# A fused attention and feed-forward kernel: two more products computed densely, and all operations in a new order

## The chip, the cores and the metric

The kernel runs on one core of a Trainium2 chip. The metric is the device time of one execution in microseconds (us), the median of several runs. A core has these engines: TensorE (PE; its weight loads are listed apart as PEld), VectorE (DVE), ScalarE (ACT), GpSimd (POOL) and SyncE (SP), which here issues nearly all DMAs. Each engine works through its own queue in the order in which the program issues instructions to it.

## The reference

```python
# q, k, v: (8, 8, 576, 64) float32; w_in: (512, 2048); w_out: (2048, 512)
theta = pi / 2 * arange(S) / S
phi(x) = concatenate([max(x, 0) * cos(theta), max(x, 0) * sin(theta)], -1)   # 128 features
kv  = einsum('bhsf,bhsd->bhfd', phi(k), v)          # per batch and head
z   = phi(k).sum(over s)
num = einsum('bhsf,bhfd->bhsd', phi(q), kv)
den = einsum('bhsf,bhf->bhs', phi(q), z)[..., None] + 1e-6
x   = (num / den) as (4608 tokens, 512)
h   = x @ w_in
out = max(0.01 * h, h) @ w_out                      # (4608, 512) float32
```

## The kernel before

**Groups.** The 4608 tokens go in nine groups of 512: group 0 to 7 hold the first 512 tokens of each of the eight batches, and group 8 the last 64 of every batch. For each group there is an attention part, a *first product* (512 tokens x 512 by 512 x 2048, with the leaky ReLU behind it) and a *second product* (512 x 2048 by 2048 x 512). All matmuls take float16 and sum in float32 in PSUM, which has eight banks of 128 x 512 values.

**Attention.** `q` and `k` steps (`q2.3.c`: group 2, token column 3, cosine) read a loaded float32 stage and write the features in float16 (L246 on DVE or POOL, L244 on ACT); `v` steps cast v. `K2` sums k times v for batch 2 into PSUM, `kv2` copies it out, `N2.j` multiplies with q, `D2.j` divides, `X2.j` (or a DMA, `Tx`) transposes to `xT`, `xc2.j` copies. `Tq` transposes q by a DMA. For the groups 0 and 1 the steps come in halves a and b, and `T`, `tc` transpose q on PE.

**Products.** A dense product is 64 matmuls of 512 columns. In group 0 the first product is dense: `M` steps (L665) and eight activations `a`. All other first products go by seven products of quarters instead of eight (Strassen's scheme in Winograd's form): `P{g}.{u}.{n}`, four units u of seven products n, each four matmuls of 256 columns (L763), 112 in all. `Xs{g}.n` (DVE) form sums of the quarters of `xT`, `Ws` those of the weights. Between the products of a unit stand the steps `b`, `s`, `u` (copies out of and into PSUM, on ACT or DVE) and `y`, `z` (sums, on DVE), and four activations `a`, `c`, `d`, `e` of half width. The second products are formed likewise: `S{g}.n` sums of the activated values G, `Tw` sums of the weights, `F{g}.{n}.{tt}.{h}` with four matmuls of 256 columns each (L852), then `t1`, `t2`, `t3`, `r` on DVE or ACT, and the stores `st`. Group 0's second product is split over its 2048 rows: the first 1024 go densely (`E{tt}.i`, L688, copied to `osb` by `ec`), the last 1024 by seven products (`F0.n.tt.1`, 56 matmuls), added to `osb` by steps `d0` and `r0`.

**Order.** The string `ORDER` lists some 1450 operations by name, with the engine behind a colon, and the program issues them in this order. `L..` are loads from memory. There are four stage buffers for q, k, v and weights in turn, so a load waits until the buffer's former content has been read. `idle.5.14.0` is 14 matmuls on zeros ahead of the real work. `split.h`, `split.n` and `join.n` change whether two PSUM banks are one tile or two.

Of the kernel before, what the change touches and what calls it, by code (L numbers as in the profile page):

```python
# [21 lines left out]
q0b.3.s:D q0a.1.s:A Lv0b k0b.7.c:D q0b.3.c:A q0a.3.s:D q0a.0.s:A q0b.2.c:P q0b.2.s:D q0a.3.c:A k0b.3.c:A
idle.4.11.1 T0.3 v0.1:A q0b.0.s:A q0a.0.c:D T0.1 k0b.0.c:P k0b.2.c:P T0.0 kp0.0.c:D q0a.2.c:P touch kp0.1.s:D
v0.0:A kp0.0.s:D kp0.1.c:D q0a.2.s:A tc0.1:D k0b.5.c:D k0b.8.c:A k0b.6.c:D tc0.0:D k0b.4.c:A kp0.2.s:D v0.3:P
Lw1.0 idle.5.2.2 K0a cw1.0:P kv0a:A v0.2:P T0.2 N0a.0 tc0.3:A tc0.2:D D0a.0 idle.5.6.3 K0b Lw1.2 Lw1.6 N0a.1
Lw1.1 Lw1.8 Lw1.3 kv0b:A N0b.0 X0a.0 D0a.1 idle.2.2.4 N0b.1 D0b.0 xc0a.0:A X0a.1 idle.2.2.5 X0b.0 M2.0.0
cw1.1:A M0.0.0 M1.0.0 M2.0.1 M0.0.1 xc0a.1:D M3.0.0 M3.0.1 xc0b.0:A D0b.1 cw1.3:D M2.1.0 Lw1.5 M2.1.1 cw1.6:P
Lw1.4 M1.0.1 cw1.2:A M3.1.0 cw1.5:P M0.1.0 M3.1.1 M0.1.1 M1.1.0 M2.0.2 X0b.1 xc0b.1:D M1.1.1 M2.0.3 M0.0.2
M0.0.3 Lq1 M1.0.2 M1.0.3 M0.1.2 cw1.4:D Lw1.7 M3.0.2 M0.1.3 M3.0.3 Ws0.1:D cw1.8:A Ws0.2:D M1.1.2 Ws0.4:D
M1.1.3 a0 M2.1.2 M4.0 Lw2.0 M2.1.3 q1.2.c:D M5.0 Lk1a M3.1.2 M3.1.3 a1 q1.0.s:D M6.0 M7.0 M6.1 M7.1 q1.1.s:D  # L30
M8.0 q1.0.c:D a3 cw1.7:D M8.1 M9.0 Lw2.1 M4.1 Lk1b M9.1 Ws0.3:D q1.3.s:A q1.3.c:A Ws1.1:D M10.0 M5.1 M10.1
M11.0 a4 q1.1.c:D M11.1 Ws1.2:D a2 M12.0 a5 cw2.0.0:D cw2.0.1:A M12.1 q1.2.s:A cw2.1.1:P M13.0 Lv1a M13.1
M14.0 M14.1 a6 M15.0 M15.1 a7 k1b.4.c:P E2.0 E2.1 E3.0 Ws1.4:D kp1.0.c:D cw2.1.0:A T1.0 T1.1 v1.0:P tc1.1:A
kp1.1.s:D E1.0 E0.0 kp1.0.s:D kp1.1.c:D Lk4n tc1.0:D T1.2 Lv1b kp1.2.s:D T1.3 k1b.0.c:A Tw1.0:D E3.1 v1.1:A
tc1.2:D k1b.5.c:P tc1.3:A E0.1 K1a Ws1.3:D k1b.7.c:P E2.2 kv1a:A S0.1h:D N1a.1 k1b.2.c:A k1b.6.c:A E2.3 N1a.0
# [5 lines left out]
P1.1.2 k2.4.c:P P1.2.1 s1.1:A P1.1.6 a1.1 c1.0 u1.1:A Tw3.1:D b1.2:D Xs1.4:D F0.1.0.1 Lq3 S0.3h:D P1.1.3
F0.1.1.1 q2.2.c:A z1.1:D Lv2 q2.0.c:D k2.3.s:A P1.0.4 Tw4.1:D P1.2.6 q2.3.s:P P1.2.2 d1.0 P1.1.7 k2.4.s:A
k2.0.s:D y1.1:D t1.0:A F0.6.0.1 u1.2:A e1.1 F0.6.1.1 t2.0:D F0.2.0.1 a1.2 k2.3.c:P s1.2:A d0.4:D d0.3:D b1.3:A
P1.2.7 P1.1.4 F0.2.1.1 z1.2:D F0.7.0.1 S0.4h:D P1.3.5 F0.7.1.1 P1.3.6 k2.2.c:A c1.1 Tq2.0 k2.1.c:A r0.2:D
P1.2.3 y1.2:D F0.5.0.1 P1.3.2 u1.3:A v2.0:A s1.3:A c1.2 F0.5.1.1 v2.1:P t3.0:D k2.1.s:P d0.5:D k2.2.s:A P1.3.7
Tq2.1 Lk3 F0.4.0.1 S1.1l:D F0.4.1.1 P1.2.4 e1.2 d1.2 r0.5:D k2.0.c:D y1.3:D c1.3 F0.3.0.1 F0.3.1.1 d1.1 P1.3.3
r0.4:D join.n Lv3 r0.3:D P1.3.4 a1.3 z1.3:D S1.2l:D e1.3 S1.1h:D K2 d1.3 F1.1.0.0 kv2:A q3.2.s:A q3.1.s:A
q3.0.s:A F1.6.0.0 F1.1.0.1 S1.3l:D N2.0 F1.1.1.0 S1.2h:D q3.0.c:P F1.1.1.1 Lv3n D2.0 F1.6.0.1 t1.1:A q3.3.s:P
F1.6.1.0 st0.2 N2.1 S1.3h:D q3.3.c:A k3.2.s:P F1.6.1.1 D2.1 F1.2.0.0 t2.1:D F1.2.0.1 st0.3 k3.3.c:A q3.1.c:A
q3.2.c:A Lk3n v3.1:P N2.2 D2.2 Tw4.0:D F1.2.1.0 k3.0.s:A F1.7.0.0 Lq4 F1.2.1.1 F1.7.0.1 N2.3 k3.1.c:A D2.3  # L50
F1.7.1.0 r1.2:A F1.7.1.1 F1.5.0.0 X2.0 k3.2.c:A X2.1 t3.1:D X2.2 X2.3 v3.0:A S1.4l:D F1.5.0.1 xc2.0:D k3.1.s:A
k3.3.s:P F1.4.0.0 xc2.1:A F1.5.1.0 S1.4h:D P2.0.1 F1.4.0.1 Lk4 xc2.2:A k3.0.c:D xc2.3:D F1.5.1.1 b2.0:A
k3.4.c:A P2.0.2 Xs2.1:D Xs2.2:D P2.0.5 P2.0.6 Xs2.3:D k3.4.s:P K3 k4.0.s:P Tq3.0 a2.0 r1.5:D u2.0:A s2.0:D
P2.1.1 kv3:A Xs2.4:D z2.0:D P2.0.7 Tq3.1 k4.0.c:D P2.0.3 k4.1.s:D k4.4.c:A F1.3.0.0 N3.0 Lv4 k4.3.c:P k4.2.s:A
F1.3.0.1 y2.0:D P2.1.5 P2.0.4 e2.0 b2.1:A q4.1.c:A D3.0 P2.1.6 s2.1:A u2.1:A q4.0.s:P N3.1 q4.3.c:D D3.1 Lv4n
P2.1.2 P2.1.3 q4.1.s:P q4.3.s:D P2.1.7 F1.4.1.0 z2.1:D d2.0 F1.3.1.0 a2.1 c2.0 y2.1:D v4.0:P P2.2.5 N3.2
k4.3.s:A e2.1 v4.1:P D3.2 P2.2.1 F1.4.1.1 P2.1.4 b2.2:A P2.2.6 k4.2.c:D s2.2:A u2.2:D N3.3 d2.1 st0.4 P2.2.2
c2.1 a2.2 P2.2.3 F1.3.1.1 P2.2.7 D3.3 st0.5 k4.4.s:A Lq5 q4.0.c:P P2.3.5 k4.1.c:A z2.2:D e2.2 y2.2:D P2.3.1 K4
S2.1l:D b2.3:A c2.2 P2.3.6 P2.3.2 u2.3:A r1.3:D Tx3 q4.2.c:A s2.3:D a2.3 S2.2l:D Tq4.0 P2.2.4 r1.4:D P2.3.7
y2.3:D F2.6.0.0 P2.3.3 F2.1.0.0 d2.2 z2.3:D q4.2.s:A P2.3.4 P3.0.1 d2.3 Xs3.1:D Xs3.2:D e2.3 c2.3 Tq4.1 b3.0:A  # L60
# [916 lines left out]
```

## Time and profile before

| what | value |
|---|---|
| median of 3 runs | 277.11 us (277.1 to 277.85) |
| profiled execution: time | 279.91 us |
| profiled execution: span from first to last instruction | 278.1 us |
| mean granted TensorE clock | 0.992 |
| busy: PE, PEld, DVE, ACT, POOL | 266.3, 232.6, 225.9, 192.9, 99.3 us |
| DMA | 57.08 MB, mean 205 GB/s |

The busy times are those of the profiled execution. Matmuls are pipelined, so a busy PE isn't PE at its peak; the step from one matmul to the next tells the rate. Times in timelines count from the first instruction.

### The profile page before, as it was taken

The numbers are of one execution on the slowest core, as the hardware profiler recorded it, in microseconds if no ns is written. First come the engines' busy times: TensorE is split into PE (matmuls) and PEld (weight loads), VectorE is DVE, ScalarE is ACT, GpSimd is POOL, SyncE is SP. The second block draws the span as 40 slices with busy tenths as digits, with TensorE's granted clock in tenths as the row PEclk, the third lists the DMA queues.
The fourth block names the chain that finished last, engine by engine and source line by source line (L and its number), as shares of the span: only waits on it lengthen the run. The fifth ranks groups of instructions, "written<-read, shape, count | busy, mean of one in ns | idle before, by whom it ended". The sixth has DMA issues, their size and how long they took to land.

```text
span 278.1 us, 7012 instructions
## 1 busy us (share of the span) xinstructions
PE 266.3 (96%) x2813; PEld 232.6 (84%) x2813; DVE 225.9 (81%) x443; ACT 192.9 (69%) x342; POOL 99.3 (36%) x72
## 2 busy tenths in 40 slices
PE   6999999699999999999999999999999999999994
PEld 2566567498889999999999899989999999999983
DVE  1987989789999899989968998879878659866752
ACT  6757998599987887777868788647755555655400
POOL 4631062899375833963544265007100000000000
PEclk9999999799999999999999999999999999999999
DMA  6999999969899999999997996694455206101224
GB/s 231 382 390 383 374 304 347 290 201 247 265 286 170 323 212 230 335 170 261 294 333 127 245 175 217 131 213 116 82 106 154 79 2 151 57 21 40 77 61 131
DMA packets 88145, 57.08 MB, mean 205 GB/s; under 512 B 53808, under 2 KB 83504, under 8 KB 87600
## 3 DMA queue, kind: packets, MB, share of 16 engines
q1 hardware_dynamic: 87504, 56.11, 74.5%
q10 hardware_dynamic: 608, 0.52, 0.7%
q8 instruction: 22, 0.36, 0.5%
q14 instruction: 11, 0.09, 0.1%
HBM read 36.70 MB, written 9.44 MB: 166 GB/s over the span
## 4 chain that ended last, share of the span: by engine, by line
PE 76%; DMA 10%; DVE 7%; ACT 3%; issue 2%; SPq 1%; DVEq 0%; ACTq 0%
PE h L763 29%; PE o L852 29%; PE h L665 4%; DMA stage<-in_q_dram 3%; DMA stage<-in_v_dram 3%; PE n L562 2%; DMA qpT<-qp 2%; DMA xT<-xs 2%; PE n L474 2%; PE n L852 2%; DVE ext L234 1%; PE h L852 1%; ACT g L783 1%; DVE xs L586 1%; DVE h L234 1%
## 5 line engine op out<-in xcount | busy, mean ns | idle before, releaser
L783 ACT ACTIVATE g<-h 128x512 f16<-128x512 f32 x90 | 51.8, 598 | 28.9 <-PE h L763 14.3
L852 PEld LDWEIGHTS <-g 128*128 128x128 f16 x680 | 65.5, 98 | 7.3 <-issue 0.4
L852 PE MATMUL o<-w,g 128*128 128x256 f16 x504 | 68.6, 273 | 0.2 <-DVE osb L234 0.2
L763 PEld LDWEIGHTS <-w 128*128 128x128 f16 x512 | 55.8, 114 | 4.9 <-issue 3.4
L763 PE MATMUL h<-xT,w 128*128 128x256 f16 x356 | 51.0, 274 | 0.0
L763 PEld LDWEIGHTS <-wext 128*128 128x128 f16 x384 | 42.1, 114 | 1.4 <-issue 0.2
L852 PE MATMUL o<-T,ext 128*128 128x256 f16 x232 | 32.9, 273 | 0.4 <-DVE osb L234 0.4
L246 POOL TENSOR_SCALAR qp<-stage,sin_t 128x512 f16<-128x512 f32 x12 | 25.1, 2096 | 15.2 <-DVE xs L586 8.8
L246 POOL TENSOR_SCALAR qp<-stage,cos_t 128x512 f16<-128x512 f32 (+1 forms) x11 | 20.1, 1832 | 28.7 <-DMA stage<-in_q_dram 20.1
L852 PEld LDWEIGHTS <-ext 128*128 128x128 f16 x272 | 26.2, 98 | 3.6 <-issue 0.6
L234 DVE TENSOR_TENSOR h<-h,u 128x512 f32<-128x512 f32 x31 | 21.5, 694 | 9.3 <-PE h L763 5.9
L763 PE MATMUL h<-X,wext 128*128 128x256 f16 x180 | 26.5, 272 | 0.2 <-ACT h L238 0.2
L246 POOL TENSOR_SCALAR kp<-stage,sin_t 128x512 f16<-128x512 f32 (+1 forms) x9 | 18.1, 2018 | 12.0 <-DMA stage<-in_k_dram 6.2
L783 ACT ACTIVATE g<-y 128x512 f16<-128x512 f32 x32 | 20.3, 635 | 2.0 <-DVE y L234 1.8
L238 ACT COPY u<-h 128x512 f32<-128x512 f32 x23 | 13.5, 589 | 11.7 <-PE h L763 11.4
L234 DVE TENSOR_TENSOR y<-h,s 128x512 f32<-128x512 f32 x29 | 19.8, 682 | 2.3 <-PE h L763 1.6
L586 DVE TENSOR_TENSOR xs<-n,rden 128x512 f16<-128x512 f32 x30 | 20.7, 691 | 1.0
L763 PE MATMUL h<-xT,wext 128*128 128x256 f16 x124 | 18.6, 273 | 0.0
L238 ACT COPY h<-h 128x512 f32<-128x512 f32 x25 | 14.5, 580 | 5.0 <-PE h L763 4.6
L852 PE MATMUL o<-ext,g 128*128 128x256 f16 x128 | 17.9, 273 | 0.0
L763 PE MATMUL h<-X,w 128*128 128x256 f16 x116 | 17.4, 272 | 0.1
L246 POOL TENSOR_SCALAR kp<-stage,cos_t 128x128 f16<-128x128 f32 (+2 forms) x12 | 16.9, 1411 | 1.1 <-DMA stage<-in_k_dram 0.8
(144 smaller groups left out, 467.0 us busy)
## 6 DMA issues: line engine op xcount, KB each, us to landing
out_dram<-osb SPq DMA_DIRECT2D x32, 256.0 KB, 3.0
stage<-in_q_dram SPq DMA_DIRECT2D x7, 1024.0 KB, 7.7
stage<-in_k_dram SPq DMA_DIRECT2D x6, 1024.0 KB, 7.1
...
```

The costliest lines, as they stand in the source:

```text
L234: eng.tensor_tensor(out=o, in0=a, in1=b, op=how)
L238: nc.scalar.copy(o, i)
L246: eng.tensor_scalar(out=o, in0=i, scalar1=0.0, scalar2=col, op0=ALU.max, op1=ALU.mult)
L474: nc.tensor.matmul(ps[:, h // NC, (h % NC) * NE : (h % NC + 1) * NE], lhsT=kps[sl, s, :], rhs=vms[sl, s, :], start=start, stop=stop, skip_ ...
L562: nc.tensor.matmul(pairs["n"][lo:hi, h // 4, (h % 4) * NE : (h % 4 + 1) * NE], lhsT=qpT[j // 2][:, j % 2, h, lo:hi], rhs=kv[b][:, h, :],)
L586: nc.vector.tensor_tensor(out=o, in0=ps[:, :, 0 : 4 * NE].rearrange("p a (b e) -> p a b e", e=NE)[:, :, :, 0:D], in1=r.rearrange("p (a b) ...
L665: nc.tensor.matmul(ps[:, m % 2, lo:hi], lhsT=w1[m // 4, c // 2][:, c % 2, m % 4 : 512 : 4], rhs=xT[0][:, lo // P : hi // P, c, :], start=( ...
L763: nc.tensor.matmul(ps[:, mi * HT : (mi + 1) * HT], lhsT=a[:, c, 2 * r0 + mi : 512 : 4], rhs=b[:, c], start=(n in (1, 5) and mi == 0 and c ...
L783: nc.scalar.activation(G[g % 2][:, m : m + 2, r * HT : (r + 1) * HT], {"a": A, "c": y22, "e": E, "d": B_}[e].rearrange("p (m t) -> p m t", ...
L852: nc.tensor.matmul(ps[:, tt], lhsT=a[:, i, tt * P : (tt + 1) * P], rhs=b[:, i], start=(first and i == at and (apart or tt == 0)), stop=(i ...
```

## The change

Group 0's second product is now wholly dense: `E{tt}.0` to `E{tt}.7`, 64 matmuls of 512 columns, copied out by `ec` and stored in four stores `st0.tt` of whole rows. Its sums `S0`, products `F0` and the steps `t`, `d0`, `r0` are gone. Group 1's first product is wholly dense as well: 64 matmuls `H{m}.{c}` and eight activations `ha`, in the two PSUM pairs `h0` and `h1` in turn; `P1`, `Xs1` and its steps in between are gone. The steps `split.n` and `join.n` go, and `split.h` comes later. The order of all operations is another one, from the first load to the last store.

```diff
 ORDER = """
-setup blank:D Lq0b q0b.0.c:P Lk0b q0b.1.s:A Lq0a idle.5.14.0 k0b.1.c:A q0b.1.c:A kp0.3.s:D q0a.1.c:A Lk0a Lv0a
...
-split.n D1b.1 Xs1.1:D cw2.2.0:A Lk2n D1b.0 X1b.1 cw2.3.0:P P1.0.1 ec1:A P1.0.5 xc1b.1:A Xs1.2:D b1.0:A Xs1.3:D
-s1.0:A P1.1.1 X1b.0 P1.0.6 P1.0.3 xc1b.0:D cw2.3.1:P q2.0.s:A P1.0.2 Lk2 u1.0:A P1.0.7 q2.3.c:A Tw1.1:D
...
+Lq0a Lk0a Lq0b setup q0a.0.c:A q0a.2.s:A blank:D q0a.0.s:A kp0.1.s:D q0b.1.c:A kp0.0.c:D kp0.0.s:D Lk0b Lv0a
...
+N0a.0 D0a.0 cw1.0:P N0a.1 K0b Lw1.8 kv0b:A idle.5.1.4 X0a.0 N0b.0 xc0a.0:A D0a.1 Lw1.3 cw1.1:A idle.2.2.5
+N0b.1 D0b.0 X0a.1 idle.4.3.6 M0.0.0 xc0a.1:D M1.0.0 M0.0.1 M2.0.0 D0b.1 X0b.0 M2.0.1 M3.0.0 xc0b.0:D M3.0.1
...
+cw2.2.0:A X1a.1 N1b.0 E1.4 E2.4 E2.5 E1.5 cw2.3.0:P xc1a.0:A D1b.0 xc1a.1:A Lk2 N1b.1 D1b.1 Ws0.2:D q2.2.c:D
+Tw1.0:D q2.0.s:D X1b.0 xc1b.0:A E0.4 E0.5 H0.0 Tw2.0:D Lk2n X1b.1 Lv2n E0.6 xc1b.1:A E2.6 cw2.3.1:A k2.0.s:D
+H0.1 H1.0 q2.3.c:D q2.3.s:D Lv2 H1.1 Lq3 E1.6 H2.0 H2.1 H3.0 ha0 H3.1 H4.0 H4.1 H5.0 ha1 Tw1.1:D Ws0.4:D
+q2.2.s:A Tw2.1:D H5.1 E2.7 k2.2.c:A ha2 H6.0 H6.1 E0.7 q2.1.s:D ec0:A E3.4 E1.7 H8.0 Ws1.2:D E3.5 H8.1 Lk3n
+k2.4.c:A H7.0 H7.1 k2.0.c:A Tw4.1:D E3.6 H9.0 k2.3.s:A q2.0.c:D ha3 H9.1 v2.0:D Ws1.4:D ha4 q2.1.c:D v2.1:D
+Ws0.3:D k2.4.s:A k2.1.c:A E3.7 H10.0 ec1:D k2.1.s:P Tw4.0:D H10.1 H11.0 ec2:A Tw3.1:D k2.3.c:D Tw3.0:D ec3:D
+st0.0 H11.1 H12.0 H12.1 H13.0 ha5 H13.1 H14.0 H14.1 k2.2.s:A H15.0 S1.1l:D Tq2.1 H15.1 ha6 K2 ha7 Tq2.0
+F1.1.0.0 F1.1.0.1 S1.3l:D S1.2l:D Ws1.3:D kv2:A Lk3 q3.1.c:A Lv3n N2.0 q3.2.s:A st0.1 F1.6.0.0 F1.1.1.0
+q3.3.s:P k3.4.s:P F1.1.1.1 S1.1h:D S1.2h:D F1.6.0.1 D2.0 S1.3h:D N2.1 q3.0.c:A F1.6.1.0 q3.0.s:P F1.6.1.1
...
 """
+    def ffn1_second(m, lo, hi, eng):
+        ps = pairs["h0" if m // 2 % 2 else "h1"]
+        for c in range(lo, hi):
+            nc.tensor.matmul(
+                ps[:, m % 2],
+                lhsT=w1[m // 4, c // 2][:, c % 2, m % 4 : 512 : 4],
+                rhs=xT[1][:, :, c, :],
+                start=(c == 0),
+                stop=(c == NKC - 1),
+            )
+
+    def relu1_second(mp, eng):
+        nc.scalar.activation(
+            G[1][:, 2 * mp : 2 * mp + 2, :], pairs["h0" if mp % 2 else "h1"], AF.Lrelu
+        )
...
     def ffn2(tt, lo, hi, eng):
         for m in range(lo, hi):
             nc.tensor.matmul(
                 bank[4 + tt],
                 lhsT=G[0][:, m, tt * P : (tt + 1) * P],
                 rhs=w2[:, m, :],
                 start=(m == 0),
-                stop=(m == NPR - 1),
+                stop=(m == NFT - 1),
             )
+    def store_tile(tt, eng):
+        rows = out[0:MAIN, :].rearrange("(p j) d -> p j d", j=J)
+        nc.sync.dma_start(rows[:, tt], osb[:, tt])
...
-        for i in range(4):
+        for i in range(8):
             op(f"E{tt}.{i}", ffn2, tt, 2 * i, 2 * i + 2)
         op(f"ec{tt}", lambda tt, eng: copy(osb[:, tt], bank[4 + tt], eng), tt)
+        op(f"st0.{tt}", store_tile, tt)
```

The steps `Xs`, `P` and those between the products now begin with group 2, and the steps `S`, `F`, `t`, `r` and the quarter stores with group 1.

More of the change, by code (lines that the diff above doesn't have):

```diff
@@ L20 @@
 ORDER = """
-setup blank:D Lq0b q0b.0.c:P Lk0b q0b.1.s:A Lq0a idle.5.14.0 k0b.1.c:A q0b.1.c:A kp0.3.s:D q0a.1.c:A Lk0a Lv0a
[L22 to L35, printed above, removed]
@@ L41 @@
[L41 to L55, printed above, removed]
@@ L56 @@
[L56 to L60, printed above, removed]
@@ L121 @@
-F8.3.0.1 r8.3.0:D st8.3.0
+Lq0a Lk0a Lq0b setup q0a.0.c:A q0a.2.s:A blank:D q0a.0.s:A kp0.1.s:D q0b.1.c:A kp0.0.c:D kp0.0.s:D Lk0b Lv0a
+idle.5.14.0 q0b.3.c:A q0b.1.s:D q0b.2.c:D q0a.3.c:A q0a.1.s:D kp0.3.s:D q0a.3.s:A k0b.6.c:D k0b.4.c:A
+k0b.3.c:A q0a.1.c:P q0b.0.s:A q0b.0.c:D k0b.2.c:D q0b.2.s:P kp0.1.c:D idle.6.6.1 T0.1 T0.0 k0b.0.c:P touch
+q0a.2.c:A Lv0b q0b.3.s:A T0.2 Lw1.0 k0b.1.c:P k0b.5.c:A v0.0:A tc0.1:A v0.1:P T0.3 tc0.0:D v0.3:P Lw1.2
+tc0.2:A kp0.2.s:D k0b.7.c:A idle.5.5.2 K0a v0.2:A Lw1.6 tc0.3:D Lw1.1 kv0a:D cw1.6:P k0b.8.c:A idle.5.2.3
@@ new lines @@
+N0a.0 D0a.0 cw1.0:P N0a.1 K0b Lw1.8 kv0b:A idle.5.1.4 X0a.0 N0b.0 xc0a.0:A D0a.1 Lw1.3 cw1.1:A idle.2.2.5
+N0b.1 D0b.0 X0a.1 idle.4.3.6 M0.0.0 xc0a.1:D M1.0.0 M0.0.1 M2.0.0 D0b.1 X0b.0 M2.0.1 M3.0.0 xc0b.0:D M3.0.1
+M1.0.1 M2.1.0 cw1.8:P Lw1.5 cw1.2:A M2.1.1 M0.1.0 Lw1.4 M3.1.0 M0.1.1 M1.1.0 cw1.3:A X0b.1 M3.1.1 M2.0.2
+M1.1.1 Lq1 M0.0.2 Lw1.7 M2.0.3 M0.0.3 M3.0.2 xc0b.1:D M1.0.2 cw1.4:D cw1.5:D M1.0.3 M0.1.2 Lw2.0 M0.1.3 M1.1.2
+M3.0.3 M1.1.3 cw1.7:D M2.1.2 M2.1.3 M3.1.2 M4.0 q1.1.s:P q1.1.c:D M5.0 a0 q1.0.s:D M3.1.3 M6.0 q1.3.s:D M7.0
@@ new lines @@
+M4.1 M5.1 Ws1.1:D a1 M6.1 M8.0 M7.1 M8.1 M9.0 M9.1 a3 q1.3.c:A M10.0 a4 M10.1 Lk1a Ws0.1:D M11.0 M11.1 Lw2.1
+M12.0 a5 q1.0.c:D cw2.0.0:D M12.1 M13.0 Lk4n Lk1b M13.1 cw2.0.1:P M14.0 a2 M14.1 M15.0 Lv1a a6 q1.2.s:A M15.1
+a7 T1.0 q1.2.c:A Lv1b v1.0:P kp1.0.s:D kp1.0.c:D E2.0 E0.0 T1.1 E0.1 E1.0 k1b.4.c:P cw2.1.1:D cw2.1.0:A
+kp1.1.c:D E1.1 tc1.1:A E2.1 E2.2 E1.2 tc1.0:D kp1.1.s:D k1b.0.c:D v1.1:A E0.2 T1.2 k1b.7.c:D k1b.3.c:D
+k1b.6.c:A E2.3 Lw2.2 k1b.5.c:P T1.3 k1b.8.c:A E1.3 tc1.2:D kp1.2.s:D K1a E3.0 kv1a:A tc1.3:D v1.2:A N1a.0 E3.1
@@ new lines @@
+t1.1:A F1.2.0.0 k3.0.c:P D2.1 N2.2 Lv3 t2.1:D F1.2.0.1 k3.1.s:P D2.2 F1.7.0.0 Lq4 F1.2.1.0 F1.2.1.1 k3.2.s:A
+k3.2.c:D q3.3.c:A k3.0.s:A q3.1.s:A N2.3 F1.7.0.1 split.h r1.2:A F1.7.1.0 D2.3 F1.7.1.1 Lk5n S1.4l:D k3.3.c:D
+X2.0 X2.1 X2.2 Tq3.0 k3.1.c:A q3.2.c:A X2.3 k3.3.s:A F1.5.0.0 k3.4.c:P F1.5.0.1 t3.1:D xc2.0:A xc2.1:D xc2.2:D
+F1.5.1.0 xc2.3:D P2.0.1 Xs2.1:D v3.0:A b2.0:A F1.5.1.1 P2.1.1 Tq3.1 P2.0.2 P2.0.5 Xs2.2:D Xs2.4:D P2.0.6
+v3.1:A K3 s2.0:A u2.0:A Xs2.3:D a2.0 z2.0:D q4.1.c:D P2.0.7 Lk4 kv3:A P2.0.3 N3.0 P2.1.5 e2.0 Lv4n y2.0:D
@@ new lines @@
+F1.4.0.0 S1.4h:D P2.0.4 b2.1:A Lv4 q4.0.c:D s2.1:A P2.1.6 d2.0 q4.0.s:P u2.1:A P2.1.2 c2.0 st0.3 k4.4.s:P
+F1.4.0.1 D3.0 st0.2 N3.1 P2.1.7 r1.5:D a2.1 F1.3.0.0 P2.2.1 z2.1:D P2.1.3 y2.1:D P2.2.5 q4.1.s:P c2.1 P2.1.4
+e2.1 F1.3.0.1 D3.1 b2.2:A k4.3.s:D N3.2 s2.2:A d2.1 P2.2.6 P2.2.3 F1.3.1.0 k4.0.s:D P2.2.2 u2.2:A F1.3.1.1
+D3.2 k4.4.c:A q4.3.c:A q4.2.s:P F1.4.1.0 a2.2 z2.2:D e2.2 N3.3 P2.3.1 k4.2.s:D P2.2.7 S2.1l:D k4.1.s:P
+k4.3.c:P b2.3:A P2.3.5 k4.1.c:A D3.3 P2.3.6 F1.4.1.1 k4.0.c:A y2.2:D s2.3:D v4.0:P P2.2.4 Lq5 r1.4:D P2.3.2
@@ L122 @@
+F8.5.1.0 S8.4l:D t3.8:D F8.5.1.1 F8.4.0.0 r8.2:A F8.4.0.1 r8.5.0:D F8.4.1.0 st7.4 r8.5.1:D F8.4.1.1 F8.3.1.0
+F8.3.1.1 F8.3.0.0 r8.4:D st7.5 F8.3.0.1 st8.2 st8.5.0 r8.3.1:D st8.5.1 st8.4 r8.3.0:D st8.3.1 st8.3.0
 """
@@ L683 @@
             op(f"a{m // 2}", relu1, m // 2)
+    def ffn1_second(m, lo, hi, eng):
[12 more added lines that the diff above has]
+        )
+    for m in range(NFT):
+        for c in range(2):
+            op(f"H{m}.{c}", ffn1_second, m, 2 * c, 2 * c + 2)
+        if m % 2:
+            op(f"ha{m // 2}", relu1_second, m // 2)
     def ffn2(tt, lo, hi, eng):
@@ L738 @@
             op(f"Ws{bp}.{n}", w1_sum, bp, n)
-        for g in range(1, NG):
+        for g in range(2, NG):
             op(f"Xs{g}.{n}", x_sum, g, n)
     LR = {"a": (0, 0), "c": (1, 1), "e": (0, 1), "d": (1, 0)}
-    FIRST_BANKS = ((4, 5, 7), (6, 3, 4), (0, 1, 6), (2, 3, 0))
     def banks(g, u):
-        if g == 1:
-            return [bank[i] for i in FIRST_BANKS[u]]
         at = 3 * (4 * g + u)
@@ L787, in relu1s @@
         )
-    for g in range(1, NG):
+    for g in range(2, NG):
         for u in range(4):
@@ L814 @@
     G_PARTS = {"l": (0, 4, 1), "h": (4, 8, 1), "e": (4, 8, 2), "o": (5, 8, 2), "x": (0, 8, 1)}
-    for g in range(NG):
+    for g in range(1, NG):
         for n in (1, 2, 3, 4):
@@ L855, in ffn2s @@
                 rhs=b[:, i],
-                start=(first and i == at and (apart or tt == 0)),
+                start=(first and i == 0 and (apart or tt == 0)),
                 stop=(i == NPR - 1 and (apart or tt == 1)),
@@ L864 @@
     QUARTER = {2: (0, 0), 5: (1, 1), 4: (1, 0), 3: (0, 1)}
-    def first_quarter(n):
-        r, c = QUARTER[n]
-        return osb[:, 2 * r : 2 * r + 2, c * HC : (c + 1) * HC]
     def half(t):
@@ L875, in store @@
         cols = slice(c * HC, (c + 1) * HC)
-        if g == 0:
-            o = first_quarter(n)
-        else:
-            o = half(osb[:, (2, 5, 4, 3).index(n)])
+        o = half(osb[:, (2, 5, 4, 3).index(n)])
         if g < B:
@@ L906, in result @@
     def result(g, n, t, eng):
-        o = first_quarter(n) if g == 0 else osb[:, (2, 5, 4, 3).index(n)]
-        if g == 0:
-            tt_op(o, half(flat(g, n)), o, ALU.add, eng)
-        elif t is None:
+        o = osb[:, (2, 5, 4, 3).index(n)]
+        if t is None:
             copy(o, flat(g, n), eng)
@@ L913, in result @@
             tt_op(o, flat(g, n), t, ALU.add, eng)
-    for g in range(NG):
+    for g in range(1, NG):
         for n in range(1, 8):
@@ L930 @@
             op(f"st{g}.{n}", store, g, n)
-            if g == 0 and t is not None:
-                op(f"d{g}.{n}", tt_op, first_quarter(n), first_quarter(n), half(t), ALU.add)
     op("split.h", change, ("h0", "h1"), 2)
-    op("split.n", change, ("n",), 2)
-    op("join.n", change, ("n",), 1)
     engines = {"": None, "D": DVE, "A": ACT, "P": POOL}
```

129 lines of the change are left out of this document (62 added, 67 removed).

## The prediction

> **What bounds the kernel now.** I read the page first, then who waited for whom on TensorE, then the stretch of the longest wait in the timelines, and last the chain through it.
>
> ```profile
> span 278.1 us, 7012 instructions
> PE 266.3 (96%) x2813; PEld 232.6 (84%) x2813; DVE 225.9 (81%) x443; ACT 192.9 (69%) x342; POOL 99.3 (36%) x72
> PEclk9999999799999999999999999999999999999999
> ```
>
> TensorE (PE) is busy for 96% of the span, so a matmul added costs its full time unless it fills a hole. One slice of the clock, the eighth (48.7 to 55.6 us), is not at full speed. The waits of PE, whole run:
>
> ```profile
> PE n L763 <- ACT u L238: 2.3, 1, 2.3
> ...
> PE n L562 <- DMA qpT<-qp: 0.6, 1, 0.6
> PE o L852 <- DVE osb L234: 0.6, 2, 0.4
> ...
> PE n L613 <- DVE xs L586: 0.2, 1, 0.2
> PE h L763 <- ACT h L238: 0.2, 1, 0.2
> ```
>
> The only long one lies in the second group's first product (L763), and it waits for a copy `u` on ScalarE (ACT). What ACT did there, and PE beside it:
>
> ```profile
> 47.61 0.59 ACT L238 COPY s<-o 128x512 f32<-128x512 f32 x1
> 51.00 0.72 ACT L244 ACTIVATE qp<-stage,sin_t 128x512 f16<-128x512 f32 x1 [2.79 <-DMA stage<-in_q_dram]
> 51.62 0.57 ACT L238 COPY u<-n 128x512 f32<-128x512 f32 x1
> ```
>
> ```profile
> 46.18 0.40 PE L598 MATMUL h<-ident,xs 128*128 128x128 f16 x4 [0.24 <-DVE xs L586]
> 46.41 0.60 PE L763 MATMUL o<-xT,w 128*128 128x256 f16 x4
> ...
> 52.24 1.01 PE L763 MATMUL n<-xT,w 128*128 128x256 f16 x4 [2.25 <-ACT u L238]
> ```
>
> `u1.0` stands in ACT's queue behind `q2.0.s`, which needs the third batch's q from memory. ACT waits 2.79 us for it, and PE 2.25 us behind ACT. The clock after the gap:
>
> ```profile
> 50.00:52.20 2.20, 0.00 (x0) 0.00 (x0) 1.11 (x2) 1.20 (x3) 1.10 (x1) 0.96 0.91 246
> 52.20:56.00 3.80, 3.76 (x21) 2.84 (x21) 3.20 (x5) 2.67 (x5) 3.80 (x3) 0.57 1.03 315
> ```
>
> For 3.8 us PE ran at 0.57 of its clock, which loses 0.43 x 3.8 = 1.6 us more than the gap itself. [...]
>
> **The price of a matmul and the size of the stage.** The chain of waits has stretches of back-to-back matmuls, and the two ends of the stage:
>
> ```profile
> 29.18 4.75 PE h L665 x22
> ...
> 41.36 9.55 DMA stage<-in_q_dram
> ...
> 70.30 1.25 PE n L474 x40
> ...
> 243.39 1.75 PE h L763 x16
> ```
>
> A 512-column matmul costs 4.75 / 22 = 0.216 us, a 256-column one 1.75 / 16 = 0.109 us. I take as the stage what lies between 46.18 us (the second group's first transposes; the products follow) and 70.30 us (L474, the sums `K2` of the third batch): 24.1 us. The old order puts all of P1 (4 x 7 x 4 = 112 matmuls of 256 columns) and F0 (7 x 2 x 4 = 56) there, and two `X1b` steps of four transposes, 0.23 us each by the step from 46.18 to 46.41. That is 168 x 0.109 + 0.46 = 18.8 us of work in 24.1 us: 5.3 us are lost, 2.3 in the gap, 1.6 to the clock, 1.4 in small waits.
>
> **The change, part by part.**
>
> Dense products: the first group's second product gets its other half dense, 32 x 0.216 = 6.9 us for F0's 6.1; the second group's first product becomes 64 x 0.216 = 13.8 us for P1's 12.2. PE's own work grows by 2.4 us. The stage then holds 6.9 + 13.8 + 0.46 = 21.2 us, after which PE turns to `K2` as before. With no wait `K2` begins at 46.18 + 21.2 = 67.4 in place of 70.30: **-2.9 us**. This is the main term, and it stands only if the 21.2 us really run dense.
>
> Why they can: P1 needed copies `b`, `s`, `u` and sums `y`, `z` between its products (20 operations on ACT and VectorE, DVE), two or three of them in a chain per unit. The dense H steps need xT, w1 and a free PSUM pair; ACT empties a pair with one `ha`. No instruction that H needs stands behind the q load of 41.36 + 9.55 = 50.9 us: ACT's queue ahead of `ha0` holds only weight casts and `xT` copies. `ha2` alone stands behind `k2.2.c`, whose load lands so:
>
> ```profile
> 44.60 1.04 SPq L289 DMA_DIRECT2D stage<-in_k_dram  x1
> ...
> DMA to landing us min/median/max: 10.1/10.1/10.1
> ```
>
> 44.6 + 10.1 = 54.7 us. H8 needs `ha2`, and 54 dense matmuls (11.7 us) with the transposes stand ahead of H8 in the stage, so PE asks for it at about 58. The cover is some 2 us. A second small wait: E0.6 needs the cast `cw2.3.0` on POOL, which in the old run starts at 47.68:
>
> ```profile
> 47.68 2.22 POOL L240 CAST w<-stage 128x1024 f16<-128x1024 f32 x2 [3.14 <-DMA stage<-in_moe_w_out_dram]
> ```
>
> It is done at 48.8, and PE arrives a little earlier. For it and for PSUM pairs returned late I take **+0.6 us** (0 to 1.5; the upper end is five waits like the small ones of 0.2 to 0.4).
>
> DVE's queue is the new cover to watch. `K2` sums into the pair `n`, which is banks 6 and 7, now held by the dense second product until `ec2` (ACT) and `ec3` (DVE). `ec3` is the 25th operation on DVE from `q2.2.c` on, which waits for 50.9; the fifth, `k2.0.s`, waits for 54.7. From there to the end of `ec3` stand 21: seven of q and k, twelve sums or copies, two casts of v. Steps of DVE with POOL quiet, then beside it:
>
> ```profile
> 26.58 0.87 DVE L246 TENSOR_SCALAR qp<-stage,sin_t 128x512 f16<-128x512 f32 x2
> 27.38 0.48 DVE L246 TENSOR_SCALAR qp<-stage,cos_t 128x512 f16<-128x512 f32 x1
> ...
> 28.37 0.68 DVE L234 TENSOR_TENSOR w<-w,w 128x1024 f16<-128x1024 f16 x1
> 28.98 0.68 DVE L234 TENSOR_TENSOR wext<-w,w 128x1024 f16<-128x1024 f16 x1
> ...
> 30.57 0.69 DVE L240 CAST w<-stage 128x1024 f16<-128x1024 f32 x1
> ```
>
> ```profile
> 58.95 0.77 DVE L246 TENSOR_SCALAR qp<-stage,cos_t 128x512 f16<-128x512 f32 x1
> 59.64 0.68 DVE L234 TENSOR_TENSOR ext<-w,T 128x1024 f16<-128x1024 f16 x1
> ```
>
> Step to step a q operation takes 0.40 alone and 0.69 beside POOL, a sum 0.61. A v cast of 1152 columns I estimate at 0.69 x 1152 / 1024 = 0.78. So `ec3` ends at 54.7 + 7 x 0.40 + 12 x 0.61 + 1.6 = 66.4, or at 68.5 with 0.69. Nearest is a mix, as the new POOL queue has but two operations there (`k2.1.s`, `q3.3.s`): about 67.4, level with PE. It hides, without reserve; no further charge, and the late end goes to the rivals.
>
> Removed with F0: four sums `S0`, three `t`, three `d`, four `r`; with P1: four `Xs1`, the 20 `between` steps. Sixteen half-width `relu1s` become eight full ones. None of it lay on PE's path except through waits already counted. Four stores by quarter become four by rows; the page's stores are 32 of 256 KB before and stay so. They pass SP's queue ahead of `Tq2`, `Lv3` and after `Lv4`; each waits for an `ec` done by 67, so nothing behind them is held: 0.
>
> Start: PE before the first matmul of the first product:
>
> ```profile
> 19.25 0.40 PE L598 MATMUL o<-ident,xs 128*128 128x128 f16 x4
> 19.48 2.09 PE L665 MATMUL h<-xT,w 128*128 128x256 f16 x16
> ...
> 21.41 0.39 PE L598 MATMUL o<-ident,xs 128*128 128x128 f16 x4
> ```
>
> Now `X0b.0` (19.25) has to come first; in the new order four matmuls stand ahead of it, and q and k halves load in another sequence with the same bytes, 33 idle matmuls for 37. Gain between 0 (the same landings decide) and 1.1, or a loss of 0.6 if a preparation falls late on its engine; nearest is the row of the transposes, so **-0.4 us**.
>
> Behind `K2`: all S1 sums now follow `ec3` on DVE. F1.6.0.0 needs the third of them, F1.6.0.1 the sixth, N2.1 the division after it. `ec3` at 67.4 + 6 x 0.61 = 71.1, the division takes a step of 1.03:
>
> ```profile
> 73.95 0.15 DVE L582 TENSOR_SCALAR den<-n 128x8 f32<-128x8 f32 x1
> ...
> 74.98 0.68 DVE L234 TENSOR_TENSOR g<-g 128x1024 f16<-128x1024 f16 x1
> ```
>
> PE with `K2` from 68.0 comes to F1.6.0.1 after 1.25, five pieces of 0.44 and a short one, near 71.7. So a wait of up to 1.5, down to none: **+0.5 us**. From there on the groups have the same matmuls and operations in another order. PE's visible waits after 56 us add up to 1.6 us (the rows above), so a better order can gain at most that; a worse one I bound by the same amount: 0, +-1.6.
>
> Sum: -2.9 + 0.6 - 0.4 + 0.5 = **-2.2 us**. The profiled run has a span of 278.1 and took 279.91; the median of the runs is 277.11. I subtract from the median: **274.9 us**.
>
> **Rivals.**
>
> *The third batch decides anyway* (no change). If the chain of its k and v is what releases `K2`, the saved stall turns into a wait there. DVE at 0.69 per q and k operation, 0.68 per sum and 1.15 per v cast (the row of ACT for that size) ends `ec3` at 54.7 + 4.8 + 8.2 + 2.3 = 70.0; with the 0.5 behind, and no gain from the start since a landing decides, that is 70.0 - 70.3 + 0.5 = +0.2: 277.3. For it: old DVE ran without a pause from 57 to 70. Against: f32 work of P1 and F0 has left that queue.
>
> ```profile
> L238 ACT CAST vm<-stage 128x1152 f16<-128x1152 f32 x2 | 2.3, 1150 | 0.0
> ```
>
> *DVE stands behind POOL* (slower). If DVE stops for the whole of a POOL operation, the two in this stretch cost 2.97 (the row below) and about 2.0: `ec3` at 66.4 + 5 = 71.4, so 71.4 - 70.3 + 0.5 = +1.6: 278.7. It decides from a mean DVE step of (70.6 - 54.7) / 21 = 0.76 us on.
>
> ```profile
> 47.74 1.26 DVE L234 TENSOR_TENSOR xT<-xT 128x512 f16<-128x512 f16 x1
> 48.92 0.41 DVE L240 COPY xT<-h 128x512 f16<-128x512 f16 x1
> ...
> 62.23 2.97 POOL L246 TENSOR_SCALAR kp<-stage,sin_t 128x512 f16<-128x512 f32 x1
> ```
>
> For it: the 1.26 us of a sum on 512 columns beside the casts of 47.68. Against: 0.77 for a q operation under POOL, and 0.67 to 0.68 for sums. [...]
>
> *Everything dense and earlier* (more gain): no new wait (-0.6), nothing behind `K2` (-0.5), the start at its best (-0.7), some of the later 1.6 regained (-0.8): 272.3.
>
> That the dense products don't remove the stall is covered by the first two.
>
> **How the numbers follow.** Forecast 0.56, more gain 0.12, third batch 0.17, POOL 0.15. A difference under 0.3% (0.8 us) can't be told from none. Faster: the first two, 0.68; same: 0.17; slower: 0.15. The likeliest case alone spans 273.3 to 276.2. The range reaches to the best case and to most of the slow one: 272.2 to 278.3.
>
> **What would show it.** The wait on `u` is gone and the eighth slice of the clock is full; L474's third batch starts near 68; PE's work in the stage is 96 matmuls of 0.216. Wrong if PE waits over 1 us at `K2` for DVE, if H waits for `ha2`, or if waits after 75 us exceed 3 us.

## The result, and the profile after

The changed kernel takes 275.7 us (median of 16 runs, 274.63 to 277.19), the kernel before on the same chip 277.76 us (16 runs, 276.46 to 280.27). The ratio is 0.9928, with a 95% interval of 0.9906 to 0.9951: 2.0 us less. The profiled execution took 274.63 us, which is the fastest of its 16 runs. Beside the experiments below the changed kernel ran eleven times more, and the one of these that was profiled took 392.2 us at a granted clock of 0.658, against 274.79 to 277.18 us for the other ten, so it is left out of their ratio, and every view of the changed kernel here is of the execution of 274.63 us. Its head:

```profile
span 272.8 us, 6773 instructions
...
PE 263.0 (96%) x2737; PEld 224.1 (82%) x2737; DVE 216.2 (79%) x432; ACT 179.4 (66%) x308; POOL 103.5 (38%) x71
...
PEclk9999999999999999999999999999999999999998
```

The eighth slice of the clock is full now. DVE has lost 9.7 us of work and ACT 13.5, the copies and sums of P1 and F0. All that the view of PE's waits lists for the changed kernel (engine, line, releaser: total, times, longest):

```profile
PE h L537 <- DVE qp L242: 2.3, 2, 1.9
PE o L374 <- DVE osb L409: 2.2, 1, 2.2
PE h L783 <- DVE u L236: 0.8, 1, 0.8
```

The first two lie ahead of the first product, so from there to the end one listed wait, of 0.8 us, is left. The wait on `u` is gone. The chain of waits of the changed kernel through the stage (start, us, what):

```profile
51.31 3.45 PE h L685 x16
54.76 0.43 PE n L707 x2
...
61.24 5.18 PE h L685 x24
66.42 1.25 PE n L470 x40
```

It is PE alone: 24 dense matmuls of H (L685) in 5.18 us are 0.216 us each, and behind them `K2` (L470) begins at 66.42, where before had 70.30 in the same view. (The timelines and the rows of stretches below give its first matmul, 66.25 and 70.14.) DVE's timeline of the changed kernel tells why nothing holds `K2` (start, us, instruction, in brackets the idle time before):

```profile
52.40 0.49 DVE L242 TENSOR_SCALAR kp<-stage,sin_t 128x512 f16<-128x512 f32 x1 [1.41 <-DMA stage<-in_v_dram]
52.80 0.92 DVE L242 TENSOR_SCALAR qp<-stage,cos_t 128x512 f16<-128x512 f32 x1
53.64 0.48 DVE L242 TENSOR_SCALAR qp<-stage,sin_t 128x512 f16<-128x512 f32 x1
54.04 0.68 DVE L230 TENSOR_TENSOR T<-w 128x1024 f16<-128x1024 f16 x1
...
63.58 0.68 DVE L236 COPY osb<-n 128x512 f32<-128x512 f32 x1
```

The first row is `k2.0.s`, the last `ec3`, which ends at 64.26, 2 us ahead of PE.

### The profile page after: what moved, and what is told of

It is laid out like the page before. It is cut to its first block, busy times and chain, and to the rows that moved or that the text cites. A ratio compares the mean times of both kernels' runs of the same rounds, so it can differ in the third digit from the quotient of the medians.

```text
span 272.8 us, 6773 instructions
## 1 busy us (share of the span) xinstructions
PE 263.0 (96%) x2737; PEld 224.1 (82%) x2737; DVE 216.2 (79%) x432; ACT 179.4 (66%) x308; POOL 103.5 (38%) x71
## 4 chain that ended last, share of the span: by engine, by line
PE 80%; DMA 14%; ACT 3%; DVE 1%; SPq 0%; issue 0%; ACTq 0%
PE o L869 30%; PE h L783 29%; DMA stage<-in_moe_w_out_dram 5%; PE h L685 5%; DMA qpT<-qp 4%; PE n L558 3%; DMA stage<-in_q_dram 2%; PE n L707 2%; PE n L470 2%; DMA xT<-xs 2%; PE o L707 2%; PE h L869 1%; PE n L869 1%; ACT qp L240 1%; PE h L458 1%; ACT qpT L234 1%
## 5 line engine op out<-in xcount | busy, mean ns | idle before, releaser
L869 PEld LDWEIGHTS <-g 128*128 128x128 f16 x640 | 61.8, 98 | 6.5
L803 ACT ACTIVATE g<-h 128x512 f16<-128x512 f32 x84 | 49.1, 598 | 26.9 <-PE h L783 16.4
L869 PE MATMUL o<-w,g 128*128 128x256 f16 x480 | 64.5, 273 | 0.0
L783 PEld LDWEIGHTS <-w 128*128 128x128 f16 x448 | 48.7, 113 | 1.9 <-issue 0.9
L242 POOL TENSOR_SCALAR qp<-stage,sin_t 128x512 f16<-128x512 f32 (+1 forms) x14 | 30.9, 2210 | 39.2 <-DMA stage<-in_q_dram 19.2
L783 PEld LDWEIGHTS <-wext 128*128 128x128 f16 x336 | 36.3, 114 | 0.5
L242 POOL TENSOR_SCALAR kp<-stage,sin_t 128x512 f16<-128x512 f32 (+1 forms) x11 | 20.8, 1895 | 18.4 <-DMA stage<-in_k_dram 16.1
L242 POOL TENSOR_SCALAR qp<-stage,cos_t 128x512 f16<-128x512 f32 (+1 forms) x11 | 22.8, 2074 | 11.5 <-DMA qpT<-qp 7.3
L230 DVE TENSOR_TENSOR osb<-o,ext 128x512 f32<-128x512 f32 x22 | 15.0, 683 | 3.0 <-PE o L869 3.0
L240 ACT ACTIVATE kp<-stage,cos_t 128x512 f16<-128x512 f32 (+2 forms) x27 | 15.3, 586 | 0.0
```

Of the source, the lines that this page charges most:

```text
L230: eng.tensor_tensor(out=o, in0=a, in1=b, op=how)
L240: nc.scalar.activation(o, i, AF.Relu, scale=col)
L242: eng.tensor_scalar(out=o, in0=i, scalar1=0.0, scalar2=col, op0=ALU.max, op1=ALU.mult)
L783: nc.tensor.matmul(ps[:, mi * HT : (mi + 1) * HT], lhsT=a[:, c, 2 * r0 + mi : 512 : 4], rhs=b[:, c], start=(n in (1, 5) and mi == 0 and c ...
L803: nc.scalar.activation(G[g % 2][:, m : m + 2, r * HT : (r + 1) * HT], {"a": A, "c": y22, "e": E, "d": B_}[e].rearrange("p (m t) -> p m t", ...
L869: nc.tensor.matmul(ps[:, tt], lhsT=a[:, i, tt * P : (tt + 1) * P], rhs=b[:, i], start=(first and i == 0 and (apart or tt == 0)), stop=(i = ...
```

## Experiments

All ratios are to the kernel before, run on the same chip beside the experiment, with a 95% interval. Line numbers shift by a few from kernel to kernel; the tiles tell which operation it is.

**How large is the stall in another execution of the kernel before?** No edit.

> The kernel before once more, for a second profile of it. Stall theory (the gain is the wait of PE for the copy u behind the q load, and the slow clock after it): PE waits for u again, but its length follows the landing of the q load; if q lands 2 us earlier than the 50.9 us of the first profile, the wait is near 0.5 us in place of 2.3, and the sums K2 begin near 68 in place of 70.3. Order theory (the gain lies at the start and behind K2, where the new order is better): K2 near 70.3 again, whatever the wait.

277.35 us, near the median of the 22 runs of that kernel on the same chip (277.59), where the execution profiled first took 279.91. PE's clock on the page of this second profile:

```profile
PEclk9999999999999999999999999999999999999999
```

And two of PE's waits in it:

```profile
PE n L763 <- DVE X L234: 0.7, 1, 0.7
PE n L763 <- ACT u L238: 0.6, 1, 0.6
```

ACT's row for `q2.0.s` in it:

```profile
49.55 0.72 ACT L244 ACTIVATE qp<-stage,sin_t 128x512 f16<-128x512 f32 x1 [1.43 <-DMA stage<-in_q_dram]
```

The same q load lets `q2.0.s` start at 49.55, in the first profile at 51.00. With it the wait on `u` shrinks from 2.25 to 0.6 us, and the slow slice of the clock is gone. `K2` begins at 67.69, 2.45 us earlier than in the first profile, which is all of the difference between the two spans (275.6 and 278.1 us). The stall is real, but its size is that of one landing, and the execution that I read had a late one. The stretch from the first matmul of the first product to `K2` shows it as a whole. One row for each execution (start and end, length, then PE busy, PEld, DVE, ACT, POOL, the clock, DMA share, GB/s); first the two profiles of before, the one shown first on top:

```profile
19.48:70.14 50.66, 47.41 (x439) 35.34 (x437) 43.89 (x82) 42.33 (x69) 27.60 (x18) 0.97 0.96 308
```

```profile
19.40:67.69 48.29, 45.98 (x440) 34.78 (x437) 44.53 (x82) 42.04 (x69) 27.23 (x18) 1.00 1.02 323
```

And the changed kernel:

```profile
18.66:66.25 47.59, 47.47 (x369) 27.59 (x368) 37.04 (x73) 32.42 (x45) 14.01 (x10) 1.00 1.05 325
```

PE stands idle for 3.25 and 2.31 us in the kernel before, for 0.12 us in the changed one. Against the second profile the changed kernel has 1.5 us more of PE's work here, 2.2 us less idle time, and starts 0.74 us earlier: 1.4 us in all.

**The change once more, beside the other kernels of this chip.** No edit.

> The changed kernel once more. Both theories: 0.990 to 0.995 of the kernel before; a second profile with K2 at 66 to 67.5 us and no wait of PE over 1 us between 20 us and the last group.

276.05 us (median of all eleven), ratio 0.9932 (0.9902 to 0.9962). The gain repeats in a second set of runs; the second profile of the stage that was asked for did not come of it.

**The wait alone, without dense products.** In the kernel before, the steps of the third batch's q that need the late load go behind `u1.1`:

```diff
-xc1b.0:D cw2.3.1:P q2.0.s:A P1.0.2 Lk2 u1.0:A P1.0.7 q2.3.c:A
+xc1b.0:D cw2.3.1:P P1.0.2 Lk2 u1.0:A P1.0.7
-a1.0 Lv2n q2.1.c:D q2.1.s:P
+a1.0 Lv2n q2.1.s:P
-u1.1:A Tw3.1:D b1.2:D
+u1.1:A q2.0.s:A q2.3.c:A Tw3.1:D q2.1.c:D b1.2:D
```

> The kernel before, with three steps of the third batch's q moved behind the second unit's copies on ScalarE and behind two weight sums on VectorE; the products stay as they were. Stall theory: the wait for u goes and the clock stays full, K2 at 67 to 69, time 274.5 to 276.5; the dense products then are not needed for this part of the gain. Order theory: no change, 277.0 to 278.5. Third: VectorE's chain of sums through this stage takes over and K2 stays at 69 to 70.5, 277 to 278.

276.64 us, ratio 0.9972 (0.9943 to 1.0002). The same stretch:

```profile
19.36:66.73 47.37, 46.06 (x439) 34.62 (x437) 43.60 (x82) 42.04 (x69) 26.63 (x18) 1.00 1.05 327
```

PE's idle time is 1.31 us instead of 2.31, and the stretch is as long as that of the changed kernel (47.37 and 47.59) with 1.4 us less of PE's work. Both rows are of executions below their kernel's median: this one took 275.57 us, 1.1 less, and the changed kernel's lies as far below. By the ratio the three moved steps bring 0.8 us, with an interval that just reaches no change; the time lies between what the two theories asked for, and `K2` at 66.73 is a little ahead of the stall theory's 67 to 69. So once the wait is gone, dense products as such make the stretch no shorter here: what they take out in idle time they put back as work.

**Where the order behind `K2` stands.** The changed kernel up to `ha7 Tq2.0`, then the order of the kernel before:

```diff
 H15.1 ha6 K2 ha7 Tq2.0
-... (order of the changed kernel)
+... (order of the kernel before)
```

> The changed kernel's order up to K2 with its dense products, then the order of the kernel before. Stall theory: it keeps the gain of the changed kernel but for what lies behind K2, 275.0 to 276.5. Order theory: most of the gain is lost, 276.8 to 278.

275.56 us, ratio 0.9927 (0.9899 to 0.9955), the same as the whole change. The stretch:

```profile
18.66:65.95 47.29, 47.29 (x370) 27.61 (x368) 36.14 (x71) 32.37 (x45) 12.67 (x10) 1.00 1.05 330
```

PE isn't idle at all. This kernel was profiled in an execution of 275.49 us, near its median: its `K2` begins 1.74 us earlier than in the second profile of before, and its span is 1.9 us shorter (273.7 and 275.6). So the whole gain lies ahead of `K2`, within the interval of some 0.8 us to either side; the new order of the remaining 207 us is worth nothing that can be measured. The time of the opposite cut (before up to `K2`, then the new order) says nothing of the new order:

> The kernel before up to K2 (with P1 and F0), then the changed kernel's order. Stall theory: 277 to 278.3, no gain beyond noise. Order theory: most of the gain, 275.5 to 276.5.

285.88 us, ratio 1.0329 (1.029 to 1.0369). Its stores of the first group stand behind steps that write the next results to `osb`, so these rows hold other values, and that is what PE waited for:

```profile
PE o L845 <- DVE osb L227: 7.4, 2, 6.9
```

The loss is one of my graft, not of the new order. Up to `K2`, though, this kernel has the order of before, and so its profile is a third one of that stretch: PE waits 0.58 us for `u`, the first product starts at 19.60 and `K2` at 67.72. The late landing of the first profile is the odd one of the three. Start of the first product and of `K2` in all profiles with one order or the other up to there (the last two differ from the changed kernel by one step before `K2` or by none, see below):

| order up to `K2` | first product, us | `K2`, us |
|---|---|---|
| before, first profile | 19.48 | 70.14 |
| before, second profile | 19.40 | 67.69 |
| before, the cut just shown | 19.60 | 67.72 |
| changed kernel | 18.66 | 66.25 |
| changed up to `K2`, then before | 18.66 | 65.95 |
| changed, `k2.2.c` first | 18.73 | 66.42 |
| changed, `Tq6.1` early | 18.25 | 65.74 |

Beside an execution without the late landing `K2` comes 1.3 to 2.0 us earlier, and 0.7 to 1.4 us of that is the earlier start.

**One dense product at a time.** First only H, with F0 kept: P1 and its steps replaced by `H`, `ha` at their places in the old order.

```diff
-P1.0.1 ec1:A P1.0.5 ... (P1, Xs1, b s u y z a c d e)
+ec1:A X1b.1 H0.0 H1.0 ... ha0 ... (H, ha; F0 in its places between)
```

> The kernel before with the second group's first product dense (H) and F0 kept; the order by hand around it, q steps behind the first two activations. Stall theory: PE's work grows by 1.6 us, the wait for u is gone, K2 near 68 to 69: 275.5 to 277.3. Order theory: 277.5 to 279, the added work and no gain.

279.02 us, ratio 1.0081 (1.005 to 1.0112): above what the stall theory asked for, and at the upper end of the order theory's range. The wait for `u` is gone. PE's longest waits behind the start:

```profile
PE h L588 <- DVE xs L576: 1.9, 2, 1.3
PE h L776 <- ACT g L796: 1.2, 1, 1.2
```

A dense H needs the whole of `xT`, and while DVE makes the last of it (`xs`) PE has nothing: in this order no other product stands there, and E is half as long. In the changed kernel the matmuls of E (L707) stand in that place. Then only E, with P1 kept: E in the new order, P1 in the sequence of the third group's P2. The hand-made order doesn't keep every shared value, so part of the output's values differ; the number and size of the instructions are those of the text.

```diff
-H0.0 H0.1 ... ha7
+P1.0.1 b1.0:A ... d1.3 c1.3 (and Xs1.1 to Xs1.4)
```

> The changed kernel with the second group's first product by seven products again (P1, its sums and copies back on ScalarE and VectorE) and the first group's second product dense; the order by hand around it. Stall theory: PE's work is 1.6 us less than in the changed kernel, but waits for copies and sums return, K2 at 68 to 71: 276.5 to 279.5. Order theory: the lower work shows, 274 to 275.3.

284.15 us, ratio 1.0256 (1.022 to 1.0291), above both expected ranges. Its waits of PE, with `K2` at 73.79:

```profile
PE h L778 <- DVE y L225: 3.3, 2, 2.6
...
PE h L778 <- ACT h L229: 2.2, 3, 1.5
PE h L778 <- ACT u L229: 1.0, 3, 0.5
```

The wholly dense E holds the banks `o` and `n` until `ec3`, so P1's units (which use `o`, `n` and `h` in the kernel before, as the rows of L763 in the prediction show) have only `h`, and each copy and sum between the products comes out as a wait. Both single-part kernels are slower than either kernel. My orders for them are made by hand, so they bound little; the two waits they show are of the parts, though: H lacks something to fill with, E takes P1's banks.

**The start alone.** The new order up to `M4.0`, then the kernel before; and the same with the q steps moved as above.

```diff
-setup blank:D Lq0b q0b.0.c:P Lk0b ... (order before, up to M4.0)
+Lq0a Lk0a Lq0b setup q0a.0.c:A ... (new order, up to M4.0)
```

> The kernel before with the changed kernel's order up to the first product's fifth block (M4.0), and its own order from there, P1 and F0 kept. In all profiles so far the first product starts at 18.7 us with the new start and 19.4 with the old. If that is worth its full time: 0.9965 to 0.9985 of the kernel before (0.4 to 1.0 us). If the stage behind waits for loads in any case: 0.999 to 1.001.

> The new start and the three q steps moved behind, P1 and F0 kept: the changed kernel's gain without its dense products. If the gain is the start and the wait for u: 0.992 to 0.9955 of the kernel before, as the changed kernel. If the dense products are needed: 0.996 to 1.0.

280.79 us, ratio 1.0119 (1.0078 to 1.0159), and 280.75 us, 1.0113 (1.0067 to 1.0159): both miss. The first product starts at 18.68, but a new wait follows. DVE's rows and PE's row of the first of the two:

```profile
28.51 0.69 DVE L233 CAST w<-ext 128x1024 f16<-128x1024 f32 x1 [4.00 <-DMA ext<-in_moe_w_in_dram]
29.12 0.68 DVE L227 TENSOR_TENSOR wext<-w,w 128x1024 f16<-128x1024 f16 x1
...
35.03 0.68 DVE L233 CAST w<-stage 128x1024 f16<-128x1024 f32 x1
...
35.77 1.82 PE L681 MATMUL n<-w,g 128*128 128x512 f16 x5 [2.63 <-DVE w L233]
```

The cast of the last weight chunk, `cw1.7`, stands early on DVE in the new start and waits 4.00 us for its load; the sums and features behind it are late, and so is a cast of the second weights that E needs (35.03). DVE in the changed kernel waits as long for that load (4.03 us, to 28.51 too), but PE doesn't wait there: the operations behind it stand in another order, with six of them ahead of the cast that E needs where this kernel has eleven, and the cast starts at 32.70. So I left `cw1.7` where before has it:

```diff
-... cw1.7:D ... M4.0 (in the new start)
+... M4.0 ... cw1.7 (at its place in the order before)
```

> The kernel before with three things of the change and none of its dense products: the order of the start (loads, casts and copies up to the first product), the two quarters of the third batch's q load issued behind the copy of u that they held up, and the cast of the last chunk of the first weights left where before has it on VectorE. Theory A (the change gains by its start, about 0.7 us, and by the wait on u that is gone, 0.6 to 2.5 us; the dense products give back what they cost): ratio 0.991 to 0.9955, first product at 18.7, second stage's first sum at 65.8 to 66.8, no wait of TensorE near 33 us. Theory B (the dense products are needed, since only with them VectorE has the time for the earlier start): ratio 0.996 to 1.0, that sum at 67.5 or later, with waits of TensorE for VectorE before it.

277.3 us, ratio 0.9993 (0.9962 to 1.0025): no gain, though M starts at 18.48 and the q steps are moved. Theory A falls; of theory B the time fits, but `K2` comes at 67.08, ahead of what it asked. So beside the new start the three moved steps show no gain, where alone they gave 0.8 us (-0.1 to 1.6). Where the 0.9 us of the start went is seen at the second batch's first sum of k times v. PE's row in this kernel, then in the second profile of before, then in the changed kernel:

```profile
38.55 0.75 PE L455 MATMUL h<-vm,kp 64*128 64x66 f16 x36 [0.64 <-POOL vm L443]
```

```profile
38.71 0.75 PE L462 MATMUL h<-vm,kp 64*128 64x66 f16 x36
```

```profile
39.90 0.74 PE L458 MATMUL h<-vm,kp 64*128 64x66 f16 x36
```

Without dense products PE comes to it 0.8 us earlier than before and waits 0.64 us for v, so 0.16 of the 0.9 us are left. The changed kernel has 22 matmuls of E between M and this sum, the other two have 14: 8 x 0.216 = 1.7 us of work whose operands are there. PE arrives at 39.90, and v, whose cast on POOL starts 1.0 us later than in the second profile of before (39.01 for 37.99), is ready at 39.68. The second half of E isn't cheaper work; here it is work that fills. That is one wait in one order: no kernel here has P1 and F0 in an order made for the new start, so that only dense products could keep the gain of the start is argued, not shown.

**How near is the cover of `ha2`, and what stands behind?** In the changed kernel the feature `k2.2.c`, which needs the third batch's k, goes ahead of `ha0` on ACT.

```diff
-H2.1 H3.0 ha0 H3.1 ... E2.7 k2.2.c:A ha2
+H2.1 H3.0 k2.2.c:A ha0 H3.1 ... E2.7 ha2
```

> The changed kernel with one step moved on ScalarE: k2.2.c, which needs the third batch's k, stands ahead of the first activation ha0, which empties a PSUM pair that H4 needs. Stall theory: H4 is asked for at 52.5 us, k lands at 52 to 55, so PE waits 1 to 3.5 us for ha0 and the clock falls behind the wait: 277 to 280. Order theory: no change against the changed kernel, 275 to 276.3.

277.5 us, ratio 1.0023 (0.9996 to 1.005). The time lies in the range of the stall theory, but by luck: the expected wait came to 0.2 us (the second row), since k landed at 51.3 us here by the transfers' view, and `K2` starts at 66.42, 0.2 us later than in the changed kernel. Most of the time is lost 100 us later (the first row):

```profile
PE n L551 <- DMA qpT<-qp: 1.9, 1, 1.9
...
PE h L678 <- ACT g L687: 0.2, 1, 0.2
```

The queue of SP in this kernel:

```profile
150.31 0.61 SPq L278 DMA_DIRECT2D stage<-in_k_dram  x1
151.03 0.51 SPq L278 DMA_DIRECT2D stage<-in_v_dram  x1
151.64 9.07 SPq L536 DMA_TRANSPOSE qpT<-qp  x1
```

and in the changed one:

```profile
149.44 0.51 SPq L285 DMA_DIRECT2D stage<-in_v_dram  x1
150.05 7.59 SPq L543 DMA_TRANSPOSE qpT<-qp  x1
```

The transpose of the seventh group's q stands behind the loads of the eighth batch; issued 1.6 us later it occupies the queue until 160.7 instead of 157.6, and PE waits. In both kernels the product that reads it starts 3.6 us after that (164.28 and 161.20), and in the changed one PE stands idle for 0.1 us ahead of it. So the changed kernel sits on an edge at that place. The profile is of an execution of 279.23 us, 1.7 above this kernel's median: against the changed kernel's profile PE is 1.25 us late at `K6`, and 4.73 us at `K7`, behind the wait. Taking the edge away didn't help:

```diff
-k6.4.c:D Lk7n ... Tq6.1 (behind Lk7n, Lk7, Lv7)
+k6.4.c:D Tq6.1 Lk7n ... (and u5.3:D ahead of Xs6.1:D, Xs6.3:D)
```

> The changed kernel with Tq6.1 issued ahead of the eighth batch's loads, and with Xs6.1 and Xs6.3 behind the copy u5.3 on VectorE; all else as it is. The changed kernel waits there for 0.3 us and 0.9 us in its profile, and 2.1 us for Tq6.1 in another. If these are on the path: 0.3 to 1.5 us less than the changed kernel, 0.988 to 0.992 of the kernel before, and a narrower spread of its runs. If PE catches up later: 0.9925 to 0.9935.

275.91 us, ratio 0.9947 (0.9917 to 0.9977), no better than the change itself. That transpose now takes 3.54 us of the queue, and the waits for it and for `u` are gone, but in the profiled execution (277.19 us, 1.3 above the median) others came (0.9 us for `xs`, 0.7 for `y`). No version beat the changed kernel by more than can be measured.

## Why the prediction was right

Forecast 274.9 us, measured 275.7; forecast -2.2 us, measured -2.0. Step by step:

- *The main term, -2.9, was over-sized, and the step that failed is that it was read off one execution and taken from the median of others.* The mechanism held: the wait on `u` is gone and the stage runs dense, with 0.1 us lost in it. Against the execution of 279.91 us the size holds too: the stretch from the first product to `K2` is 50.66 - 47.59 = 3.1 us shorter. But the 2.3 us of stall and 1.6 us of slow clock belong to that execution. Against the one of 277.35 us, near the median, the stretch is 0.7 us shorter, or 1.0 in the kernel cut at `K2`.
- *The added work of +2.4 us is there:* 96 x 0.216 for 168 x 0.109. The rows of the stretch show only +1.5 us of PE's busy time. The rest is probably the modelled end of the last matmul ahead of a gap, which counts as busy: four matmuls are given 0.60 us where their steps take 4 x 0.109 = 0.44, and the second profile of before has six gaps in the stretch (6 x 0.16 = 1.0), the changed kernel one.
- *The +0.6 for E0.6 and the pairs of H was not incurred:* no wait of PE between 18.66 and 66.25.
- *The start, -0.4, was -0.8* (18.66 for 19.48): the row of the transposes was too small a bound for the likeliest value. In the one order tried without the longer E it did not pay (the last start experiment).
- *`ec3` at 67.4 was too late by 3.1 us.* The step of 0.40 for features and 0.60 for sums held, beside POOL too but for the feature at 52.80; the mistake was the release, 54.7 by before's load, 52.40 in the changed kernel, whose k load is issued earlier (42.83 for 44.60). From `k2.0.s` to the end of `ec3` it is 11.9 us, by the forecast's two sums 11.7 and 13.8.
- *Behind `K2` +0.5 was not incurred,* as `ec3` was early. *The rest, 0 +-1.6, is 0* within what the runs can tell: the cut at `K2` shows it.

So beside a median run the stage was given 2.9 - 0.7 = 2.2 us too much, and 0.6 + 0.5 + 0.4 = 1.5 us of charges and start were off the other way. The mechanism was right; that the sum came within 0.8 us of the measured median with these sizes is luck. What stays open: the changed kernel's own profile is of its fastest run, 1.1 us under its median, so of the 2.8 us between its span and that of the second profile of before 1.4 lie behind `K2`, where the medians show nothing. The kernel cut at `K2`, profiled near its median, accounts for 1.7 of the 2.0 us up to `K2`. The rest lies within what single executions differ by, and no run here tells it apart. How the gain divides between the dense products and the order ahead of `K2` is open too: the two single parts and the starts without dense products were slower or no faster, but all of them in orders made by hand.

Of the rivals, *the third batch decides* fell, since DVE was done 2 us ahead of PE at `K2`. *DVE stands behind POOL* fell by this row of POOL in the changed kernel:

```profile
52.51 2.24 POOL L242 TENSOR_SCALAR kp<-stage,sin_t 128x512 f16<-128x512 f32 x1 [5.38 <-DMA stage<-in_k_dram]
```

By these times, which the profile gives only roughly for POOL, DVE did two features and a sum in the 2.24 us (52.80, 53.64 and 54.04 in the rows above); the first took 0.92 us for 0.48, the other two were not slower. The sum, which reads two slices of a weight tensor, ran its 0.68 us beside the POOL feature, and the whole price was 0.44 us. Another POOL operation cost more: beside a POOL cast (1.44 us from 31.05 on) a feature of DVE took 1.26 us at 31.51 in the same kernel, as a sum did at 47.74 in the kernel before. *More gain* fell with the size of the main term.
